# Cached attention with a token mixer: each bulk load split by columns over the SyncE and ScalarE queues

## The chip, the cores and the metric

The kernel runs on one core of a Trainium2 chip. The metric is the device time of one execution in microseconds (us); the time of a kernel is the median of several executions. Beside it stands one profiled execution, from which every duration here is taken. Its span runs from the first to the last recorded instruction.

## What is computed

One decoding step of grouped-query attention over caches of keys and values, plus a token-mixing MLP, plus the input itself. All data is 32-bit float.

```
x: (8, 1, 512)     k_cache, v_cache: (8, 8, 8192, 128)     wq: (512, 4096)     wo: (4096, 512)
xn = layernorm(x)
q  = (xn @ wq) as (8, 32 heads, 1, 128)          # four heads share one key/value head
p  = softmax(q . k * 128**-0.5)
A  = concat(p . v) @ wo
B  = w2 . gelu(layernorm(xn) . w1 + b1) + b2     # S = 1: 1792 hidden units for each of the 512 channels
out = x + A + B
```

The caches hold 64 pairs (batch, key/value head); the kernel works on two of them at a time. A "pair load" of K or V is 128 rows of 64 KB, 8.39 MB; there are 32 of K and 32 of V, and 8.39 MB each of `wq` and `wo`.

## The kernel before

**Buffers.** One tile `raw` holds five slots of 32 KB in each of 128 rows (`RING`). K of step n takes two neighbouring slots: slots 1 and 2 for an even n, 0 and 1 for an odd n (`home`, line 103; steps 0 and 1 differ). V takes slots 3 and 4. In the last step V goes into slots 2 and 1 as two loads, `wo`'s low half into slot 0 and its high half into slot 3.

**A step.** For each of K's two slots, `score_half` (line 420) lets VectorE transpose it in place (`turn`, line 293) and TensorE multiply it with the queries (`scores`, line 302). `softmax_and_values` (line 427) then runs: TensorE multiplies the *previous* step's probabilities with its V (`values`, line 340) around a maximum and an exponential of the current scores (`exps`, ScalarE, line 322), V of the current step is asked for, and `send_on` (line 328) turns the probabilities. `take` (line 347) copies the finished sums from PSUM to `ob` on ScalarE; `place` (line 361) picks the wanted blocks from `ob` on TensorE. In the loop (14 rounds of two steps), each step also runs four Gelus of the mixer on ScalarE (line 394), with their weighting on GpSimd (lines 397 to 400).

**Order.** The schedule is written by hand: each engine runs its instructions in the order in which the Python code issues them. All bulk loads are begun by SyncE (`load`, line 122; `load_wo`, line 143; `wq` at line 97). SyncE has no other work in the program but the store of the result. A load waits, on the engine that begins it, until its slots are free.

**Semaphores of loads.** The framework deals eight semaphores (`DMAHW0` to `DMAHW7`) in turn to the loads of the program, one to each; a load that is dealt a semaphore again waits until the load that had it before has landed, where no earlier wait says so already. A load in the loop has its own, and V of the odd steps counts on a semaphore of the kernel, `landed`, which TensorE waits for (line 430).

**The end.** The code of the last step, whose parts the change touches:

```python
    load(vc, n, 1, 1)
    load_wo(0)
    softmax_and_values(n, lambda: load_wo(1))
    take(n - 1)
    total(HALF)
    place(OT[HALF:, :, final], HALF, 0, 1)
    sums = ps_a.tile([P, D], F32, name="acc")
    values(LAST, 0)
```

`load_wo(1)` begins five loads of 8, 4, 2, 1 and 1 of the 32 chunks of `wo` (a chunk is 128 rows of 2 KB, 0.26 MB). After `values(LAST, 1)`, `take` and `place` of the last step, TensorE multiplies 28 chunks (line 512), ScalarE copies the sums (line 514), TensorE adds the last four chunks (line 520), VectorE copies the result (line 527), and SyncE stores it.

Of the kernel before, what the change touches and what calls it, by code (L numbers as in the profile page):

```python
# [51 lines left out]
def attn_mixer_kernel(ctx: ExitStack, tc: tile.TileContext, x, kc, vc, wq, wo, w1, b1, w2, b2, out):  # L52
    nc = tc.nc
# [10 lines left out]
    def slot(at, n=1):  # L64
        return slots[:, at:at + n, :]
# [12 lines left out]
    def misc():  # L78
        return ps_m.tile([P, 512], F32, name="misc")
# [10 lines left out]
    nc.scalar.dma_start(x_sb, x.rearrange("b s d -> (b s) d"))  # L90
    b2t = const.tile([B, 1], F32, name="b2t")
    nc.scalar.dma_start(b2t, bass.AP(tensor=b2.tensor, offset=b2.offset, ap=[[0, B], [1, 1]]))
    body = slot(2, 2).rearrange("p s m -> p (s m)")
    rows = wq.rearrange("(p e) n -> p (e n)", p=P)
    for a in range(2):
        half = slice(a * QE * QN // 2, (a + 1) * QE * QN // 2)
        nc.sync.dma_start(body[:, half], rows[:, half])
    nil = const.tile([P, 1], F32, name="nil")
    nc.vector.memset(nil, 0.0)

# [10 lines left out]
    landed = tc.alloc_semaphore("landed")  # L111

    def load(c, i, at, part=None, own=False):
        flat = pairs[id(c)]
        if isinstance(i, int):
            rows = flat[i].rearrange("(p m) -> p m", p=P)
        else:
            rows = flat[bass.ds(i, 1)].rearrange("a (p m) -> p (a m)", p=P)
        n = 1 if part is not None else 2
        if part is not None:  # L120
            rows = rows[:, part * SIZE:(part + 1) * SIZE]
        d = nc.sync.dma_start(slot(at, n).rearrange("p s m -> p (s m)"), rows)
        if own:
            d.then_inc(landed, 16)
            tc.no_tile_sem_insts.add(d.ins.name)
            tc.add_to_no_dep_group("landed", d.ins)
        return d

    def tile_at(a):
        return slots[:, a, :].rearrange("p (t d) -> p t d", d=DH)  # L130
# [6 lines left out]
    def load_wo(high):  # L137
        t = slot(3 if high else 0).rearrange("p s (c n) -> p (s c) n", n=D)
        rows = wo.rearrange("(p c) n -> p c n", p=P)
        at = 0  # L140
        for n in WO_HIGH if high else (NWO // 2,):
            o = high * NWO // 2 + at
            nc.sync.dma_start(t[:, at:at + n], rows[:, o:o + n])  # L143
            for c in range(n):
                WO[o + c] = t[:, at + c]
            at += n
# [5 lines left out]
    for k in range(2):  # L152
        load(kc, 0, k, k)
# [22 lines left out]
    m = misc()  # L176
# [16 lines left out]
    rows = tmp[:, :2 * REP]  # L193
# [7 lines left out]
    for k in range(2):  # L201
        for a in range(NB):
            o = a * W + a // 2 * HW
# [3 lines left out]
    for c in range(NCH):  # L207
        for s in range(2):
            o = s * HW + c * REP
# [20 lines left out]
    for k in range(PER):  # L230
        js = slice(k * MJ, (k + 1) * MJ)
        for t, src in ((tabs[:, k::PER, 0], w1t), (tabs[:, k::PER, 1], b1t), (tabw[:, k::PER], w2t)):
            n = len(range(k, ROUNDS, PER))
# [9 lines left out]
    for k in range(2):  # L243
        t = const.tile([P, CH_T * W + W], F32, name=f"pt{k}")
# [12 lines left out]
    def q_project():  # L257
        ms = [misc(), misc()]
        for e in range(QE):
            for h in range(HKV):  # L260
                g = h % NB
                nc.tensor.matmul(ms[h // NB][g * W:(g + 1) * W, :], lx[:, e, :],  # L262
                                 body[:, e * QN + h * REP * DH:e * QN + (h + 1) * REP * DH],
                                 start=(e == 0), stop=(e == QE - 1))
        load(kc, 1, home(1))
        load(vc, 0, 4, 0)
        for a in range(2):
            q = big()
            nc.scalar.copy(q, ms[a])
            mt = misc()  # L270
            for r in range(REP):
                nc.tensor.transpose(mt[:, r * P:(r + 1) * P], q[:, r * DH:(r + 1) * DH], ident)
            nc.vector.tensor_copy(QT[:, a * NB:(a + 1) * NB].rearrange("p g b r -> p r g b"),
                                  mt.rearrange("p (r g x) -> p r g x", r=REP, x=W)[:, :, :, :B])
# [32 lines left out]
    def top(n):  # L307
        mr = work.tile([P, 1], F32, name="mr")
        nc.vector.tensor_reduce(mr, SD[n], AX.X, ALU.max)  # L309
        return mr  # L310

    def exps(n, mr):
        m = misc()
        nc.tensor.transpose(m[:, :P], mr.to_broadcast([P, P]), ident)  # L314
        t = big()[:, :P]
        nc.vector.tensor_tensor(t, m[:, :P], hmask, op=ALU.add)  # L316
        nb = work.tile([P, 1], F32, name="nb")
        nc.vector.tensor_reduce(nb, t, AX.X, ALU.max)
        ns = work.tile([P, 1], F32, name="ns")
        nc.vector.tensor_scalar(ns, nb, -SCALE, None, op0=ALU.mult)  # L320
        p = big()
        nc.scalar.activation(p, SD.pop(n), AF.Exp, bias=ns, scale=SCALE, accum_out=lr[:, n % PER:n % PER + 1])  # L322
        return p

    def send_on(p):
        for k in range(2):
            m = misc()
            nc.tensor.matmul(m, send[:, k, :], p, start=True, stop=True)  # L328
            nc.vector.transpose(PT[k][:, :CH_T * W], m)  # L329

    def apart(d):
        tc.declare_no_dep(d.ins, group="landed", across_iterations=True, reason="waits on landed instead")

    def values(n, k, own=False):
        if not k:
            OD[n] = ps_a.tile([P, 512], F32, name="acc")
        v = tile_at(VAT.get(n, (3, 4))[k]).rearrange("p (c t) d -> p t c d", c=NCH)
        for t in range(CH_T):
            j = t % NB
            d = nc.tensor.matmul(OD[n][j * W:(j + 1) * W, :].rearrange("p (c d) -> p c d", c=NCH),  # L340
                                 PT[k][:, t * W:(t + 1) * W], v[:, t],
                                 start=(not k and t < NB), stop=(k == 1 and t >= CH_T - NB))
            if own:
                apart(d)

    def take(n):
        nc.scalar.copy(OB[:, n % PER, :], OD.pop(n))  # L347
# [79 lines left out]
    def softmax_and_values(n, then, ready=None):  # L427
        mr = top(n)
        if ready is not None:
            nc.tensor.wait_ge(landed, 16)  # L430
            nc.tensor.sem_inc(landed, -16)
        if n:
            values(n - 1, 0, ready is not None)
        p = exps(n, mr)
        if n:
            values(n - 1, 1, ready is not None)
        d = then()
        if ready is not None:
            apart(d)
        send_on(p)  # L440

# [3 lines left out]
    score_half(1, True)  # L445
    load(kc, 2, home(2))
    softmax_and_values(0, lambda: None)
    warm()

    score_half(1, False)  # L450
    softmax_and_values(1, lambda: load(vc, 1, 3))
    nc.tensor.sem_inc(landed, 16)
    take(0)
    total(0)
    q_set(FIRST)
# [5 lines left out]
    with tc.For_i(0, ROUNDS, 1, iteration_sync=SYNC) as r:  # L461
        for k in range(PER):
            n = FIRST + k
            score_half(n, True)
            load(kc, r * PER + (n + 1), home(n + 1))
            score_half(n, False)
            softmax_and_values(n, lambda: load(vc, r * PER + n, 3, own=(k == PER - 1)), k == 0 or None)
            take(n - 1)
            if not k:
                place(RES[:, :, bass.ds(r, 1)], 0)  # L470
                mx_end(r * B)
                mx_begin(r)
                mx_now(r)
            else:
                total(0)
                q_set(r * PER + 2 * FIRST)
            for j in range(k * MIX[0], k * MIX[0] + MIX[k]):
                mx_step(j)
            warm()

    final = slice((B - 1) * BS, (B - 1) * BS + 1)
    n = LAST - 1
# [11 lines left out]
    n = LAST  # L494
    score_half(n, True)
    load(vc, n, 2, 0)
    score_half(n, False)
# [5 lines that stand above are left out]
# [7 lines left out]
    for c in range(FOLD):  # L510
        o = c % NB * W
# [44 lines left out]
```

## Time and profile before

| | us |
|---|---|
| median of 3 executions (lowest, highest) | 1285.84 (1285.82, 1285.96) |
| the profiled execution | 1286.04 |
| its span | 1284.2 |
| TensorE matmuls busy | 767.5 |
| VectorE busy | 696.9 |
| ScalarE busy | 228.8 |
| GpSimd busy | 248.1 |
| bytes moved | 553.86 MB, 431 GB/s over the span |

The profiled execution is 1.84 us longer than its span (work before the first and after the last record), and 0.20 us above the median. Busy times of the engines overlap each other; the transfers run on 16 DMA engines, of which the profile gives the mean busy share.

### The profile page before, as it was taken

To read this page: it belongs to the slowest core of one execution; us is meant where nothing else is said; L and a number is where in the kernel's file an instruction comes from. 1 tells how busy PE (TensorE), PEld (TensorE's weight loads), DVE (VectorE), ACT (ScalarE), POOL (GpSimd) and SP (SyncE) were. 2 spreads that over 40 slices of the span, in tenths; PEclk is the share of its full clock that TensorE was granted. 3 is DMA by queue.
4 is the path that set the end of the run, shared out by engine and by line. 5 is a ranking of instruction groups with operands and counts; after the bars stand their busy time and mean duration, and the time that the engine had idled before them with its cause. 6 is when DMAs were issued, how large, how long until landed. Compare 5 with 4: busy or idle time off the path is not lost. (4 is left out here: it accounts for less than half of the span.)

```text
span 1284.2 us, 13214 instructions
## 1 busy us (share of the span) xinstructions
PE 767.5 (60%) x4830; PEld 170.9 (13%) x4830; DVE 696.9 (54%) x615; ACT 228.8 (18%) x382; POOL 248.1 (19%) x244
## 2 busy tenths in 40 slices
PE   4367556576465665556666475765656665464677
PEld 1111111111011111111111011110111110011112
DVE  3666644466654465644466554565644466543661
ACT  0000221212222121221212222121221211222000
POOL 1000221202222022221212222022221212222000
PEclk8788787887777897788787777877778887778888
DMA  9999999999999999999999999999999999999998
GB/s 409 425 442 425 448 427 433 445 429 433 425 447 429 431 447 427 433 433 439 431 429 447 427 433 445 429 433 427 445 431 429 447 427 433 439 433 431 430 431 354
DMA packets 10975, 553.86 MB, mean 431 GB/s; under 512 B 1324, under 2 KB 1356, under 8 KB 1748
## 3 DMA queue, kind: packets, MB, share of 16 engines
q1 hardware_dynamic: 10836, 553.67, 99.6%
q8 instruction: 8, 0.13, 0.0%
q10 hardware_dynamic: 32, 0.02, 0.0%
q0 software_dynamic: 96, 0.02, 0.0%
q14 instruction: 3, 0.02, 0.0%
HBM read 553.69 MB, written 0.02 MB: 431 GB/s over the span
## 5 line engine op out<-in xcount | busy, mean ns | idle before, releaser
L293 DVE STREAM_TRANSPOSE raw<-raw 128x2048 f32<-128x2048 f32 x256 | 565.4, 2275 | 232.8 <-DMA raw<-in_A_k_cache_dram 218.6
L302 PE MATMUL acc<-raw,z 128*32 128x512 f32 x2048 | 372.8, 815 | 433.9 <-DVE raw L293 385.7
L340 PE MATMUL acc<-raw,pt 128*32 128x512 f32 x2048 | 245.5, 621 | 10.9 <-DMA raw<-in_A_v_cache_dram 5.5
L399 POOL TENSOR_TENSOR g<-g,noww 128x512 f32<-128x512 f32 x98 | 101.8, 1039 | 376.2 <-ACT g L394 376.2
L302 PEld LDWEIGHTS acc<-raw,z 128*32 128x32 f32 x2048 | 47.0, 124 | 737.7 <-DVE raw L293 550.9
L322 ACT ACTIVATE t2k<-acc,ns 128x512 f32<-128x512 f32 x32 | 22.0, 687 | 603.2 <-PE acc L340 525.5
L394 ACT ACTIVATE g<-hb,nows 128x512 f32<-128x512 f32 x112 | 87.5, 782 | 192.8 <-POOL macc L400 175.4
L329 DVE STREAM_TRANSPOSE pt<-misc 128x512 f32<-128x512 f32 x64 | 45.9, 717 | 126.0 <-PE misc L328 121.6
L397 POOL TENSOR_TENSOR macc<-g,noww 128x512 f32<-128x512 f32 x14 | 14.5, 1038 | 515.8 <-ACT g L394 515.8
L400 POOL TENSOR_TENSOR macc<-macc,g 128x512 f32<-128x512 f32 x84 | 106.4, 1267 | 6.6
L340 PEld LDWEIGHTS acc<-raw,pt 128*32 128x32 f32 x2048 | 66.0, 114 | 174.7 <-issue 150.0
L316 DVE TENSOR_TENSOR t2k<-misc,hmask 128x128 f32<-128x128 f32 x32 | 9.3, 292 | 114.8 <-PE misc L314 114.8
L328 PE MATMUL misc<-t2k,send 128*128 128x512 f32 x128 | 65.1, 632 | 3.1 <-ACT t2k L322 3.1
L394 ACT ACT_TABLE_LOAD x28 | 35.9, 1283 | 94.5 <-PE hb L385 94.3
L309 DVE TENSOR_REDUCE mr<-acc 128x1 f32<-128x512 f32 x32 | 22.1, 690 | 52.9 <-PE acc L302 52.9
L409 ACT ACT_TABLE_LOAD x28 | 35.9, 1283 | 0.5
L347 ACT COPY ob<-acc 128x512 f32<-128x512 f32 x32 | 18.7, 585 | 74.3 <-PE acc L340 74.3
L328 PEld LDWEIGHTS misc<-t2k,send 128*128 128x128 f32 x128 | 22.0, 191 | 45.2 <-issue 41.9
L405 PE MATMUL misc<-macc,esel 128*8 128x512 f32 x30 | 15.3, 590 | 19.6 <-DVE esel L403 19.6
L385 PE MATMUL hb<-hn,hsel 8*128 8x512 f32 x28 | 18.9, 761 | 12.9 <-DVE hsel L384 12.9
L406 DVE TENSOR_TENSOR yrow<-misc,yrow 8x512 f32<-8x512 f32 x16 | 10.9, 679 | 19.2 <-PE misc L405 19.2
L262 PE MATMUL misc<-raw,lend 128*32 128x512 f32 x64 | 12.5, 953 | 11.3 <-DMA raw<-in_A_wq_dram 11.3
(99 smaller groups left out, 195.4 us busy)
## 6 DMA issues: line engine op xcount, KB each, us to landing
raw<-in_A_v_cache_dram SPq DMA_DIRECT2D x4, 4096.0 KB, 34.3
raw<-in_A_wq_dram SPq DMA_DIRECT2D x2, 4096.0 KB, 17.0
raw<-in_A_k_cache_dram SPq DMA_DIRECT2D x2, 4096.0 KB, 30.8
raw<-in_A_wo_dram SPq DMA_DIRECT2D x1, 4096.0 KB, 26.4
raw<-in_A_wo_dram SPq DMA_DIRECT2D x1, 2048.0 KB
raw<-in_A_wo_dram SPq DMA_DIRECT2D x1, 1024.0 KB, 29.9
raw<-in_A_wo_dram SPq DMA_DIRECT2D x1, 512.0 KB
raw<-in_A_wo_dram SPq DMA_DIRECT2D x2, 256.0 KB, 30.8
```

The source lines that it names most:

```text
L293: nc.vector.transpose(t, t)
L302: nc.tensor.matmul(SD[n][c * W:(c + 1) * W, :].rearrange("p (t j) -> p t j", j=W), Z[:, n % PER, q, (1 - k) * REP:(1 - k) * REP + W], t[:, ...
L309: nc.vector.tensor_reduce(mr, SD[n], AX.X, ALU.max)
L322: nc.scalar.activation(p, SD.pop(n), AF.Exp, bias=ns, scale=SCALE, accum_out=lr[:, n % PER:n % PER + 1])
L328: nc.tensor.matmul(m, send[:, k, :], p, start=True, stop=True)
L329: nc.vector.transpose(PT[k][:, :CH_T * W], m)
L340: d = nc.tensor.matmul(OD[n][j * W:(j + 1) * W, :].rearrange("p (c d) -> p c d", c=NCH), PT[k][:, t * W:(t + 1) * W], v[:, t], start=(not ...
L385: nc.tensor.matmul(hb, hsel.to_broadcast([B, P]), hn, start=True, stop=True)
L394: nc.scalar.activation(g, hb7 if last else hb, AF.Gelu_apprx_tanh, bias=nows[:, 1, j:j + 1], scale=nows[:, 0, j:j + 1])
L399: nc.gpsimd.tensor_tensor(g, g, w, op=ALU.mult)
L400: nc.gpsimd.tensor_add(acc7 if last else acc, acc7 if last else acc, g)
L409: nc.scalar.activation(small.tile([P, 1], F32, name="warm"), nil, AF.Exp)
```

## The change

Each bulk load becomes two loads of half of its columns, for all 128 rows. The first half is begun by SyncE, the second by ScalarE, by a new helper:

```diff
+    def begin(dst, src):
+        n = dst.shape[1] // 2
+        return [eng.dma_start(dst[:, x], src[:, x]) for eng, x in ((nc.sync, slice(0, n)), (nc.scalar, slice(n, 2 * n)))]
...
-        nc.sync.dma_start(body[:, half], rows[:, half])
+        begin(body[:, half], rows[:, half])
...
-        d = nc.sync.dma_start(slot(at, n).rearrange("p s m -> p (s m)"), rows)
-        if own:
+        ds = begin(slot(at, n).rearrange("p s m -> p (s m)"), rows)
+        for d in ds if own else ():
...
-            nc.sync.dma_start(t[:, at:at + n], rows[:, o:o + n])
+            begin(*(x.rearrange("p c n -> p (c n)") for x in (t[:, at:at + n], rows[:, o:o + n])))
...
-            nc.tensor.wait_ge(landed, 16)
-            nc.tensor.sem_inc(landed, -16)
+            nc.tensor.wait_ge(landed, 32)
+            nc.tensor.sem_inc(landed, -32)
```

For a pair load, half of the columns is one slot: SyncE loads the lower slot, ScalarE the upper one. Lines of the changed kernel below the helper are four higher (`take` is at 351), and the loads all have line 95.

ScalarE at the end of the program, before (the last two steps; `t2k` are probabilities, `ob` what `take` writes):

```order
L322 ACTIVATE t2k,lr<-acc,ns 128x512 [waits DVE_49,PE_49,Activation_49]
L347 COPY ob<-acc 128x512 [waits PE_49]
L409 ACTIVATE warm<-nil 128x1
L322 ACTIVATE t2k,lr<-acc,ns 128x512 [waits DVE_49,PE_49]
L347 COPY ob<-acc 128x512 [waits PE_49,Activation_49] x2
L514 COPY t2k<-acc 128x512 [waits DVE_49,PE_49]
```

The same place in the changed kernel, from the last step's V loads on:

```order
L95 DMA raw<-in_A_v_cache_dram 128x4096 [waits DMAHW1_49]
L95 DMA raw<-in_A_v_cache_dram 128x4096 [waits DMAHW5_49,DVE_49,PE_49]
L95 DMA raw<-in_A_wo_dram 128x4096 [waits DMAHW4_49,DVE_49,PE_49]
L326 ACTIVATE t2k,lr<-acc,ns 128x512 [waits DVE_49]
L95 DMA raw<-in_A_wo_dram 128x2048 [waits DMAHW7_49,DMAHW6_49,PE_49]
L95 DMA raw<-in_A_wo_dram 128x1024 [waits DMAHW1_49]
L95 DMA raw<-in_A_wo_dram 128x512 [waits DMAHW3_49]
L95 DMA raw<-in_A_wo_dram 128x256 [waits DMAHW6_49]
L95 DMA raw<-in_A_wo_dram 128x256 [waits DMAHW7_49]
L351 COPY ob<-acc 128x512 [waits PE_49,Activation_49] x2
L518 COPY t2k<-acc 128x512 [waits DVE_49,PE_49]
```

Eight loads now stand among ScalarE's instructions there. The second halves of `load_wo(1)` stand between the last exponential and the two `take` copies, and four of them wait for a DMA semaphore alone.

TensorE at the end of the kernel before, from the `place` that reads the first of those two copies:

```order
L361 MATMUL misc<-ob,pick 32x128 [waits DVE_49,Activation_49]
L361 MATMUL misc<-ob,pick 32x128 x3
L340 MATMUL acc<-raw,pt_190 32x512 [waits DMAHW5_49]
L340 MATMUL acc<-raw,pt_190 32x512 x15
L506 MATMUL acc<-yrow,spread 32x512
L340 MATMUL acc<-raw,pt_192 32x512 [waits DMAHW6_49,DVE_49]
```

and of the changed kernel:

```order
L365 MATMUL misc<-ob,pick 32x128 [waits DVE_49,Activation_49]
L365 MATMUL misc<-ob,pick 32x128 x3
L344 MATMUL acc<-raw,pt_194 32x512 [waits DMAHW1_49,DMAHW0_49]
L344 MATMUL acc<-raw,pt_194 32x512 x15
L510 MATMUL acc<-yrow,spread 32x512
L344 MATMUL acc<-raw,pt_196 32x512 [waits DMAHW3_49,DMAHW2_49,DVE_49]
L344 MATMUL acc<-raw,pt_196 32x512 x15
L365 MATMUL misc<-ob,pick 32x128 [waits Activation_49]
L365 MATMUL misc<-ob,pick 32x128 x3
L516 MATMUL acc<-raw,ot 32x512 [waits DMAHW4_49,DVE_49]
L516 MATMUL acc<-raw,ot 32x512 x7
L516 MATMUL acc<-raw,ot 32x512 [waits DMAHW5_49]
```

Nothing moved on TensorE; what changed is what its rows wait for. The rows also show how the semaphores were dealt: 0 and 1 to the last V's first part, 2 and 3 to its second part, 4 and 5 to the low half of `wo`. The next rows wait for 6 and 7 (the 8 chunks), 0 and 1 (the 4 chunks), 2 and 3 (the 2 chunks), and 4, 6, 5, 7 (the single ones).

In the loop, ScalarE's round before begins with the even step's exponential, `take` and the mixer's tables (`nows`):

```order
L322 ACTIVATE t2k,lr<-acc,ns 128x512 [waits PE_I-451_own,DVE_I-451_own,Activation_I-451_own,Activation_49]
L347 ISA
L347 COPY ob<-acc 128x512 [waits PE_I-451_own,Activation_I-451_own]
L388 ISA
L388 COPY nows<-tabs 128x16 [waits Activation_I-451_own,Pool_49]
```

and in the changed kernel:

```order
L95 DMA raw<-in_A_k_cache_dram 128x8192 [waits DMAHW1_I-460_own,DVE_I-460_own,DMAHW5_I-460_own,PE_I-460_own,DMAHW0_49]
L326 ISA
L326 ACTIVATE t2k,lr<-acc,ns 128x512 [waits PE_I-460_own,DVE_I-460_own,Activation_I-460_own,Activation_49]
L95 ISA
L95 DMA raw<-in_A_v_cache_dram 128x8192 [waits DMAHW3_I-460_own,PE_I-460_own,DMAHW3_49]
L351 REGISTER_ALU
L351 COPY ob<-acc 128x512 [waits Activation_I-460_own]
```

The upper half of the next K stands ahead of the exponential, the upper half of V between it and `take`; the Gelus and the table loads follow. The odd step has the same order.

More of the change, by code (lines that the diff above doesn't have):

```diff
@@ L126, in load @@
             tc.add_to_no_dep_group("landed", d.ins)
-        return d
+        return ds
     def tile_at(a):
@@ L436, in softmax_and_values @@
             values(n - 1, 1, ready is not None)
-        d = then()
-        if ready is not None:
+        ds = then()
+        for d in ds if ready is not None else ():
             apart(d)
@@ L451, in attn_mixer_kernel @@
     softmax_and_values(1, lambda: load(vc, 1, 3))
-    nc.tensor.sem_inc(landed, 16)
+    nc.tensor.sem_inc(landed, 32)
     take(0)
```

## Prediction

> **What bounds the kernel now.** I read the page's DMA lines first, then busy time by stretches, then the chain of waits' end. The page:
>
> ```profile
> DMA  9999999999999999999999999999999999999998
> ...
> q1 hardware_dynamic: 10836, 553.67, 99.6%
> ...
> L293 DVE STREAM_TRANSPOSE raw<-raw 128x2048 f32<-128x2048 f32 x256 | 565.4, 2275 | 232.8 <-DMA raw<-in_A_k_cache_dram 218.6
> ```
>
> SyncE's queue q1 keeps the 16 DMA engines busy for 99.6% of the span, from the first slice to the last. VectorE, the first to touch a K load, waits 218.6 us for them. So the engines wait for transfers, and the compute is hidden under them. One round of the loop (two steps) as a stretch, the last number being GB/s, and SyncE's issues in one round, then the two places around it:
>
> ```profile
> 1000.00:1077.30 77.30, 46.22 (x298) 9.97 (x290) 42.81 (x36) 15.37 (x25) 17.32 (x16) 0.81 1.00 434
> ```
>
> ```profile
> 575.74 0.33 SPq L122 DMA_DIRECT2D raw<-in_A_k_cache_dram  x1
> 594.27 0.33 SPq L122 DMA_DIRECT2D raw<-in_A_v_cache_dram  x1
> 614.08 0.33 SPq L122 DMA_DIRECT2D raw<-in_A_k_cache_dram  x1
> 653.01 0.33 SPq L122 DMA_DIRECT2D raw<-in_A_k_cache_dram  x1
> ```
>
> A round takes 653.01 - 575.74 = 77.27 us for four pair loads, 19.3 us each at 434 GB/s. How early the queue is filled:
>
> ```profile
> raw<-in_A_k_cache_dram SPq DMA_DIRECT2D x31, 28.2
> ```
>
> A K load lands 28.2 us after its issue; 19.3 us of that is its own transfer, so about 9 us of earlier transfers still stand in the queue at each issue. That is the reserve by which an issue may be late before the DMA engines run dry.
>
> The last part of the chain that ended last, in order of time:
>
> ```profile
> 1249.57 30.87 DMA raw<-in_A_wo_dram
> 1280.44 0.04 issue
> ```
>
> The last piece of `wo` lands at 1280.44, and 3.8 us later the span (1284.2) ends. The transfers bound the kernel up to there, and very little compute is left behind them.
>
> **The change part by part.** *Rate of the loop.* Bytes stay the same; rows halve from 64 to 32 KB. The trace has loads of 32 KB rows: the two loads of K at step 0.
>
> ```profile
> 32.44 8.89 DVE L293 STREAM_TRANSPOSE raw<-raw 128x2048 f32<-128x2048 f32 x4 [17.87 <-DMA raw<-in_A_k_cache_dram]
> 42.09 8.89 DVE L293 STREAM_TRANSPOSE raw<-raw 128x2048 f32<-128x2048 f32 x4 [0.28 <-DMA raw<-in_A_k_cache_dram]
> ```
>
> VectorE was released by the first at 32.44 and by the second at 42.09: 9.65 us for 4.19 MB, 434.6 GB/s, the rate of the 64 KB rows. So the smaller rows and the more frequent completions cost nothing that shows. Two queues busy at once are in no stretch of this trace. A gain is bounded by the 0.4% that q1 leaves, 0.4% of 1284.2 = 5.1 us; I take the same for a loss, and zero as the value, since the row that is nearest shows the same rate. The Trainium skill (DMA: Bandwidth & Descriptors, section Where 436 GB/s comes from) gives a ceiling of 435.2 GB/s for these transfers, which by estimate leaves 1284.2 x (1 - 434/435.2) = 3.5 us to be gained, not 5.1.
>
> *ScalarE as an issuer in the loop.* ScalarE in the round shown above:
>
> ```profile
> 569.08 0.20 ACT L409 ACTIVATE warm<-nil 128x1 f32<-128x1 f32 x1
> 594.25 0.58 ACT L347 COPY ob<-acc 128x512 f32<-128x512 f32 x1 [1.90 <-PE acc L340]
> 613.34 0.20 ACT L409 ACTIVATE warm<-nil 128x1 f32<-128x1 f32 x1
> ```
>
> ScalarE's last work of a step ends at 569.28, 6.5 us before K's slots were free (575.74), and at 613.54, 0.5 us before 614.08. Its K halves can thus be begun no later than SyncE began the whole load. V's half stands behind the exponential, which waits for scores anyway, and ahead of `take`, which waits for the same `values` as the load. SyncE's halves come earlier than before: the lower K slot of an odd step is free since the step before, and the lower V slot after the first half of `values`. With equal turns both queues stay filled; no gap arises, and none was there to close. The cost is 0.33 us of issue ahead of each `take`; what waits for `take` in an even step is `place`, then VectorE's turn of the next K:
>
> ```profile
> 603.93 17.66 DVE L293 STREAM_TRANSPOSE raw<-raw 128x2048 f32<-128x2048 f32 x8 [3.87 <-DMA raw<-in_A_k_cache_dram]
> ```
>
> VectorE stood 3.87 us idle for K there, which hides 0.33. Uncovered it would be 28 x 0.33 = 9 us. Loop: 0.
>
> *The start.* The first loads on ScalarE stand ahead of the square root of the layer norm, and one of them (K of step 0, upper slot, second half) is dealt the semaphore of the first piece of `wq`, so it waits until that has landed.
>
> ```profile
> 3.61 0.29 ACT L167 ACTIVATE sd<-mv,epst 8x1 f32<-8x1 f32 x1 [0.65 <-DVE mv L165]
> 13.40 6.06 PE L262 MATMUL misc<-raw,lend 128*32 128x512 f32 x32 [7.98 <-DMA raw<-in_A_wq_dram]
> 22.80 6.47 PE L262 MATMUL misc<-raw,lend 128*32 128x512 f32 x32 [3.34 <-DMA raw<-in_A_wq_dram]
> ```
>
> Half of `wq` had landed by 13.40, and a quarter no later. The root then starts at about 15 instead of 3.61, and the query projection about 2 us behind it, at 17, not 13.40; it ends its first half at about 23.2, and the second, held by `wq` until 22.80 anyway, 0.4 us later than before. K's next load is queued until 42 at least, so 0.4 us is hidden. Start: 0.
>
> *The end.* Here a wait is added whose cover I can't find. SyncE's queue shows how a waiting load treats what is behind it:
>
> ```profile
> 1.66 28.01 SPq L122 DMA_DIRECT2D raw<-in_A_k_cache_dram  x3
> 29.71 21.53 SPq L122 DMA_DIRECT2D raw<-in_A_v_cache_dram  x2
> ```
>
> The third K load waits for the projection, and the V load behind it, whose slot 4 nothing had used, begins only at 29.71. A load that waits holds its engine's later instructions. The Trainium skill (Perfetto Trace Analysis, section DMA Instruction — HWDGE) puts a load's wait on the issuing sequencer ahead of its next decode, and the row agrees.
>
> By ScalarE's order at the end, the two single-chunk halves wait for semaphores 6 and 7. The holders of these before them are the halves of the 8 chunks. Behind them stand both `take` copies. The first `take` releases TensorE's `place`, and behind that on TensorE stands all the rest: both parts of the last `values`, the projection with `wo`, the sum. When do the 8 chunks land? Rows of the end:
>
> ```profile
> 1251.58 0.58 ACT L347 COPY ob<-acc 128x512 f32<-128x512 f32 x1 [1.91 <-PE acc L340]
> 1254.28 3.60 PE L340 MATMUL acc<-raw,pt 128*32 128x512 f32 x29
> 1257.81 1.04 PE L506 MATMUL acc<-yrow,spread 8*32 8x512 f32 x2
> 1261.14 5.12 PE L340 MATMUL acc<-raw,pt 128*32 128x512 f32 x32 [2.29 <-DMA raw<-in_A_v_cache_dram]
> 1266.38 0.58 ACT L347 COPY ob<-acc 128x512 f32<-128x512 f32 x1 [14.22 <-PE acc L340]
> 1267.02 1.06 PE L361 MATMUL misc<-ob,pick 128*32 128x128 f32 x8 [0.76 <-ACT ob L347]
> 1268.92 0.21 DVE L367 TENSOR_TENSOR ot<-s,rl 32x32 f32<-32x32 f32 x1
> 1270.80 8.24 PE L512 MATMUL acc<-raw,ot 128*32 128x512 f32 x56 [2.72 <-DMA raw<-in_A_wo_dram]
> ```
>
> ```profile
> L143 SPq DMA_DIRECT2D raw<-in_A_wo_dram x6: 327/440/458, 1244.3 to 1249.6; - x6
> ```
>
> The low half of `wo` landed at 1270.80, the last of the 16 high chunks at 1280.44, so 8 of them take 4.82 us: 1275.62. However the queues share, both halves of these 8 land no earlier than 4.82 us before all transfers end, since only 8 chunks follow them. Two issues of 0.44 us follow: the first `take` begins at 1276.6 instead of 1251.58. From there, with no transfer left to wait for:
>
> `take` to the end of `place` takes 1.70 (1266.38 to 1268.08). The first part of `values`, on a TensorE that idled for over 20 us, takes 5.33 by the first row below; the row above has 3.60 for 29 when it had been working. Line 506 takes 1.0, the second part of `values` 3.64, also below. `take`, `place` and VectorE's steps of the last V take 2.87 (1266.26 to 1269.13). Line 512 has 56 at the pace of 29 in 3.60, 6.95. From its end to the span's end it is 5.16 as before (1279.04 to 1284.2).
>
> ```profile
> 584.89 5.33 PE L340 MATMUL acc<-raw,pt 128*32 128x512 f32 x32 [0.76 <-PEq L431]
> 1247.82 3.64 PE L340 MATMUL acc<-raw,pt 128*32 128x512 f32 x32
> ```
>
> Sum: 1276.6 + 1.70 + 5.33 + 1.0 + 3.64 + 2.87 + 6.95 + 5.16 = 1303.3 us of span, 19.1 above before. What was spread over 1251 to 1270 beside the transfers now comes behind them. With 1.84 us around the span and 0.20 down from the profiled execution to the median, the time is 1304.9.
>
> Ends of these terms: both parts at 3.64, line 506 at 0.6, line 512 at 56 x 3.64/32 = 6.4 and 4.9 behind it give 1300.3; 5.33, 5.12, 8.24 and 5.16 give 1306.1. As times 1301.9 and 1307.7.
>
> **The rivals.** *Only transfers count, and the wait holds nothing* (no change). ScalarE would have to pass `take` ahead of waiting loads. For it: the bytes and the rate stay, as in all rows above. Against it: the V load held until 29.71. Time: 1285.84, give or take the 5.1 of the rate. The Trainium skill (DMA: Bandwidth & Descriptors, section Rules for kernel authors) says that spreading loads over issuers doesn't help bandwidth, as all share 16 engines; by that rule alone the time stays, and the 434.6 beside 434 agrees. It decides if `take` begins before 1257.5: from there the 26.7 us of the chain above end at 1284.2.
>
> *Finer release pays* (faster). SyncE's halves are begun earlier and fill q1's missing 0.4%, and the end isn't held: 1285.84 - 5.1 = 1280.7. Against it: both conditions, the second as above; a gain of 5.1 alone leaves 1299.8.
>
> *Two busy queues cost rate* (slower still). The one stretch in which ScalarE's and GpSimd's small loads ran beside SyncE's:
>
> ```profile
> 2.00:12.00 10.00, 0.61 (x4) 0.55 (x4) 7.76 (x39) 1.26 (x2) 2.22 (x6) 1.00 0.96 402
> ```
>
> 402 against 434 GB/s, though the first loads' latency is in it. If that held throughout, transfers would take 8% or 102 us more: 1407. Against it: 0.04 MB of small loads can hardly slow 4 MB by themselves.
>
> **How the numbers follow.** The held `take`: 0.88; no change: 0.03; faster: 0.02; a lost rate beyond 0.4%: 0.07. Forecast 1304.9. Range: 1301.9 and 1307.7, widened by 5.1 either way: 1297 to 1313. Changes within 0.2% (2.6 us) can't be told from none here. Slower 0.95, same 0.03, faster 0.02.
>
> **What would show it.** Right: the round still takes 77.3 us; the first `take` of the end (line 351) starts near 1276 with the single-chunk halves on ScalarE just before it; TensorE has a gap of over 20 us from about 1254 on; DMA share falls to nothing in the last 23 us of the span; the chain that ended last runs through ScalarE's queue into lines 365, 344 and 516. Wrong: `take` still near 1252; rounds off 77.3 by over 0.3 us; or waits of VectorE for K that grow while the DMA share falls.

## The result and the profile after

The changed kernel takes 1307.32 us (median of four executions, 1305.95 to 1308.32), the kernel before beside it 1285.83 (1285.70 to 1285.96): a ratio of 1.0166, with a 95% interval of 1.0149 to 1.0184. That is 21.5 us more. The profiled execution took 1307.2 us, its span 1305.4.

The page of the changed kernel, its DMA lines and two groups (busy time and mean on the left of the last bar, idle time before them and its cause on the right):

```profile
DMA  9999999999999999999999999999999999999992
GB/s 401 431 437 434 433 433 434 434 432 433 434 432 433 434 432 434 433 433 434 434 433 432 433 433 434 434 434 434 434 434 434 434 434 434 434 433 433 431 424 119
...
q1 hardware_dynamic: 10836, 276.85, 49.2%
q10 hardware_dynamic: 10832, 276.85, 49.2%
...
L297 DVE STREAM_TRANSPOSE raw<-raw 128x2048 f32<-128x2048 f32 x256 | 565.4, 2275 | 191.2 <-DMA raw<-in_A_k_cache_dram 176.6
...
L365 PE MATMUL misc<-ob,pick 128*32 128x128 f32 x256 | 19.0, 280 | 22.1 <-ACT ob L351 22.1
```

The bytes are split evenly over SyncE's queue (q1) and ScalarE's (q10), and together they need twice as many packets, 21668 for the same 553.7 MB. The DMA engines stay busy until the last slice, which was 8 before and is 2 now, so most of that slice (32.6 us wide) has no transfers. VectorE's idle time for K is less than before (176.6 us, it was 218.6), although the kernel is longer: it isn't where the time went. The idle time of `place` (line 365), 22.1 us behind ScalarE's copy, is where an engine shows the loss.

The bulk of the program as one stretch, before and then after (the last number is GB/s):

```profile
121.00:1180.00 1059.00, 637.09 (x3996) 137.59 (x3995) 580.70 (x482) 212.14 (x346) 236.62 (x219) 0.80 1.00 434
```

```profile
121.00:1180.00 1059.00, 645.77 (x3972) 139.07 (x3964) 580.55 (x481) 210.47 (x344) 233.57 (x215) 0.80 1.00 433
```

One GB/s is the last digit shown, so I went to SyncE's issues of even-step K loads twelve rounds apart, before and then after:

```profile
227.74 0.33 SPq L122 DMA_DIRECT2D raw<-in_A_k_cache_dram  x1
...
1155.02 0.33 SPq L122 DMA_DIRECT2D raw<-in_A_k_cache_dram  x1
```

```profile
227.64 0.33 SPq L95 DMA_DIRECT2D raw<-in_A_k_cache_dram  x1
...
631.25 0.33 SPq L95 DMA_DIRECT2D raw<-in_A_v_cache_dram  x1
632.38 0.33 SPq L95 DMA_DIRECT2D raw<-in_A_k_cache_dram  x1
...
1157.05 0.33 SPq L95 DMA_DIRECT2D raw<-in_A_k_cache_dram  x1
```

Twelve rounds took 927.28 us before and 929.41 after: 77.27 and 77.45 us a round, 0.23% more. By these loads a single round before takes anything from 76.39 to 78.16 us, but three together take 231.79 to 231.84, and 232.35 or 232.36 after, so the difference is clear of this spread. The two rows in the middle show that SyncE begins the lower K slot of an odd step 1.13 us behind a V load, early, as the code says; the rounds are no shorter for it.

The end of the changed kernel as a timeline (start, duration, engine, line; in brackets the idle time before and what ended it):

```profile
1253.83 0.33 ACTq L95 DMA_DIRECT2D raw<-in_A_wo_dram  x1
...
1255.76 23.32 ACTq L95 DMA_DIRECT2D raw<-in_A_wo_dram  x4
...
1258.22 0.23 PE L357 MATMUL misc<-lr,ohg 128*32 128x1 f32 x4
...
1279.17 0.59 ACT L351 COPY ob<-acc 128x512 f32<-128x512 f32 x1 [24.65 <-DMA raw<-in_A_wo_dram]
...
1279.81 1.27 PE L365 MATMUL misc<-ob,pick 128*32 128x128 f32 x5 [21.37 <-ACT ob L351]
...
1281.52 5.18 PE L344 MATMUL acc<-raw,pt 128*32 128x512 f32 x29
...
1287.59 3.64 PE L344 MATMUL acc<-raw,pt 128*32 128x512 f32 x32
...
1291.36 0.59 ACT L351 COPY ob<-acc 128x512 f32<-128x512 f32 x1 [11.60 <-PE acc L344]
...
1294.16 6.21 PE L516 MATMUL acc<-raw,ot 128*32 128x512 f32 x56 [1.10 <-DVE ot L371]
```

ScalarE begins the half of the 8 chunks at 1253.83 and needs from 1255.76 to 1279.08 to begin the four loads behind it. Only then does `take` start, at 1279.17; before, it started at 1251.58. TensorE stands from 1258.45 to 1279.81. The chain that ended last, at that place:

```profile
1253.83 24.89 DMA raw<-in_A_wo_dram
1278.74 0.33 ACTq L95
1279.17 0.60 ACT ob L351
```

It names the wait: the half of the 8 chunks lands at 1278.74, the last single-chunk load, which was dealt the same semaphore, is begun then, and `take` follows 0.43 us later. Nobody reads those 8 chunks before 1294.16. Two stretches of the end (busy time of TensorE, its weight loads, VectorE, ScalarE and GpSimd; then the clock granted to TensorE, with 1.00 for full speed, DMA share, GB/s):

```profile
1260.00:1279.00 19.00, 0.00 (x0) 0.00 (x0) 0.00 (x0) 0.00 (x0) 0.00 (x0) 0.52 1.00 423
1284.00:1305.40 21.40, 15.81 (x159) 5.59 (x151) 1.16 (x4) 1.17 (x2) 0.00 (x0) 0.98 0.01 2
```

For 19 us no engine computes while transfers run; then for 21.4 us the engines compute while no transfers run. The two used to lie over each other.

### The profile page after: what moved, and what is told of

The parts are those of the page before. It is cut to its first block, busy times and chain, and to the rows that moved or that the text cites. A ratio compares the mean times of both kernels' runs of the same rounds, so it can differ in the third digit from the quotient of the medians.

```text
span 1305.4 us, 13503 instructions
## 1 busy us (share of the span) xinstructions
PE 778.9 (60%) x4830; PEld 173.4 (13%) x4830; DVE 696.9 (53%) x615; ACT 228.8 (18%) x382; POOL 248.3 (19%) x244
## 2 busy tenths in 40 slices
DMA packets 21776, 553.88 MB, mean 424 GB/s; under 512 B 2524, under 2 KB 3068, under 8 KB 3588
## 3 DMA queue, kind: packets, MB, share of 16 engines
q1 hardware_dynamic: 10836, 276.85, 49.2%
## 5 line engine op out<-in xcount | busy, mean ns | idle before, releaser
L297 DVE STREAM_TRANSPOSE raw<-raw 128x2048 f32<-128x2048 f32 x256 | 565.4, 2275 | 191.2 <-DMA raw<-in_A_k_cache_dram 176.6
L344 PE MATMUL acc<-raw,pt 128*32 128x512 f32 x2048 | 260.2, 652 | 33.8 <-DMA raw<-in_A_v_cache_dram 28.5
L313 DVE TENSOR_REDUCE mr<-acc 128x1 f32<-128x512 f32 x32 | 22.1, 690 | 51.6 <-PE acc L306 51.6
L365 PE MATMUL misc<-ob,pick 128*32 128x128 f32 x256 | 19.0, 280 | 22.1 <-ACT ob L351 22.1
L368 DVE TENSOR_TENSOR t2k<-misc,keep 64x128 f32<-64x128 f32 (+1 forms) x17 | 4.8, 284 | 36.7 <-PE misc L365 36.7
```

Source lines behind the costliest of these rows:

```text
L297: nc.vector.transpose(t, t)
L365: nc.tensor.matmul(m[at + k * W:at + (k + 1) * W, :DH], pick[:, c, :], OB[:, k, c * DH:(c + 1) * DH], start=(c == 0), stop=(c == NCH - 1))
```

## The experiments

**The theory:** some 18 us are the held `take`, and what is left over, about 3 us, is lost in the transfers. **The rivals:** the loss comes from two queues that disturb each other; or it comes from the finer release of slots or from ScalarE's issues in the loop. For the 3 us there were further candidates: shorter rows (more packets), or more loads. Every kernel below ran beside the kernel before, which took 1286.08 beside the first three and the kernel with one queue, 1286.39 beside the three with fewer pieces and the one with the 64-byte gap, and 1285.95 beside the 1 KB gap and the last two.

### Both halves kept, but nothing of the end waits on ScalarE

Here only `load_wo(1)` changes against the changed kernel; all other loads stay halved over both engines.

```diff
-            begin(*(x.rearrange("p c n -> p (c n)") for x in (t[:, at:at + n], rows[:, o:o + n])))
+            if high:
+                nc.sync.dma_start(t[:, at:at + n], rows[:, o:o + n])
+            else:
+                begin(*(x.rearrange("p c n -> p (c n)") for x in (t[:, at:at + n], rows[:, o:o + n])))
```

> The change, but the high half of wo is again five whole loads begun by SyncE, so no load stands among ScalarE's instructions between the last exponential and the two take copies. Theory A (the held take costs about 19 us, the two queues themselves 0.2% of rate): take starts near 1256, a median of about 1288.5. Theory B (two queues, smaller rows or more loads cost 1.6% of the rate throughout): about 1306, with take near 1279 or the loop's rounds over 78 us. Theory C (the held take is all): 1286.

Measured: 1288.93, ratio 1.0022 (1.0013 to 1.0031). The first `take` in the timeline, and the end of the chain:

```profile
1258.60 0.59 ACT L354 COPY ob<-acc 128x512 f32<-128x512 f32 x1 [1.97 <-PE acc L347]
```

```profile
1262.88 20.49 DMA raw<-in_A_wo_dram
1283.37 0.04 issue
```

`take` waits for TensorE again, and the kernel ends with its transfers, at 1283.37 where they ended at 1280.44 before. Of the 21.5 us, 18.6 are gone (21.49 less 2.85).

### All loads and waits kept, but `take` moved off ScalarE

The edit above also removes loads. This one leaves each load where it is and moves the two last copies to VectorE.

```diff
-    def take(n):
-        nc.scalar.copy(OB[:, n % PER, :], OD.pop(n))
+    def take(n, vector=False):
+        (nc.vector.tensor_copy if vector else nc.scalar.copy)(OB[:, n % PER, :], OD.pop(n))
...
-    take(n - 1)
+    take(n - 1, True)
...
-    take(LAST)
+    take(LAST, True)
```

> The change with all its loads and waits, but the two take copies of the end run on VectorE, which has no loads in its queue. Theory A: the waits of the single-chunk halves stay, but nothing stands behind them that TensorE needs before 1283; the first copy starts near 1256, a median of about 1289 (0.2% of rate, and the last single-chunk halves land about 3 us late as they are begun late). Theory B: about 1307, the chain's end is moved only by the rate.

Measured: 1289.28, ratio 1.0025 (1.0015 to 1.0035). From its timeline:

```profile
1255.54 23.42 ACTq L95 DMA_DIRECT2D raw<-in_A_wo_dram  x4
...
1259.91 0.65 DVE L351 COPY ob<-acc 128x512 f32<-128x512 f32 x1
...
1261.52 3.60 PE L344 MATMUL acc<-raw,pt 128*32 128x512 f32 x29
```

ScalarE's queue stands as long as in the changed kernel, 23.42 us, and it costs nothing, since nothing needed stands behind it until the sums are copied at 1282.15. So neither the wait nor the second queue is the price: what stood behind the wait was.

### The kernel before, with only that wait added

```diff
+    nc.scalar.copy(small.tile([P, 1], F32, name="hold"), WO[NWO // 2][:, :1])
     take(n - 1)
```

One small copy on ScalarE reads the first of the 8 chunks, and so can't start before they have landed. No load is touched.

> The kernel before, all loads whole and on SyncE, plus one ScalarE copy of one column (0.2 us) out of the 8 chunks of wo, put ahead of the first take of the end, so that take waits for those 8 chunks. Theory A: they land at 1275.6 as worked out from the trace of before; take starts at 1275.9, and with the 26.2 us from take to the end that the changed kernel showed the span is 1302.1, the median 1303.7. Theory B (the loss is in the two queues): 1286, as the chain would be hidden again.

Measured: 1304.18, ratio 1.0137 (1.0122 to 1.0153).

```profile
1276.41 0.19 ACT L501 COPY hold<-raw 128x1 f32<-128x1 f32 x1 [25.23 <-DMA raw<-in_A_wo_dram]
1276.51 0.58 ACT L347 COPY ob<-acc 128x512 f32<-128x512 f32 x1
```

The wait alone costs 18.1 us. With the 3.2 us that the kernel with `take` on VectorE keeps, that makes 21.3 of the 21.5.

### Fewer pieces, so that the last load waits for something earlier

If the dealt semaphore is the cause, the number of pieces sets what the last one waits for. With pieces of 8 and 8 the last half has the semaphore of the last V's first part; with 8, 4, 4 that of V's second part; with 8, 4, 2, 2 that of the low half of `wo`; with the changed kernel's five that of the 8 chunks.

```diff
-WO_HIGH = (8, 4, 2, 1, 1)
+WO_HIGH = (8, 8)
```

> The change with the high half of wo in two pieces of 8 chunks instead of five (8, 4, 2, 1, 1). ScalarE's last half then waits for the semaphore of the last V's first part, which by the changed kernel's trace lands about three times 8 chunks and two parts ahead of 1278.7, near 1254.6. Theory A: take is not held (about 1258.6, as with the high half whole), and the end pays only for a last piece of 8 chunks: the transfers end at 1283.5, then 4 chunks of line 516 (1.2 us) and 5.2 us: span 1289.9, median about 1291.5. If the number of loads or the queue's order were the cost instead of the held take: 1305 to 1307.

> The change with the high half of wo in pieces of 8, 4 and 4 chunks. ScalarE's last half waits for the last V's second part, which lands near 1264.3. Theory A: take at 1264.8, and 26.2 us from there to the end: span 1291.0, median about 1292.6. A theory in which the hold is hidden up to some point would put it at 1289.

> The change with the high half of wo in pieces of 8, 4, 2 and 2 chunks. ScalarE's last half waits for the low half of wo, which lands near 1274.0. Theory A: take at 1274.5, span 1300.7, median about 1302.3. Any theory without the held take: as with 8, 4, 4 or lower.

Measured, in this order: 1291.64, ratio 1.0039 (1.0024 to 1.0055); 1293.78, ratio 1.0057 (1.0041 to 1.0072); 1302.79, ratio 1.0131 (1.0115 to 1.0146). The first `take` with 8 and 8:

```profile
1257.71 0.59 ACT L351 COPY ob<-acc 128x512 f32<-128x512 f32 x1 [1.97 <-PE acc L344]
```

with 8, 4, 4 (the last load just before it):

```profile
1264.95 0.33 ACTq L95 DMA_DIRECT2D raw<-in_A_wo_dram  x1
1265.38 0.58 ACT L351 COPY ob<-acc 128x512 f32<-128x512 f32 x1 [9.60 <-DMA raw<-in_A_v_cache_dram]
```

and with 8, 4, 2, 2:

```profile
1255.64 18.83 ACTq L95 DMA_DIRECT2D raw<-in_A_wo_dram  x3
...
1274.57 0.58 ACT L351 COPY ob<-acc 128x512 f32<-128x512 f32 x1 [20.38 <-DMA raw<-in_A_wo_dram]
```

The releaser in the brackets changes from TensorE to V to `wo`, as the deal has it. From the start of `take` to the end of the span it is 25.9 us with 8, 4, 4 (span 1291.3), 26.4 with 8, 4, 2, 2 (1301.0), 26.2 in the changed kernel and 26.5 with the wait alone (1303.0). Where `take` starts late, the end follows it at nearly the same distance. With 8 and 8 it isn't held, and the chain of that kernel goes through its last load:

```profile
1254.19 28.41 DMA raw<-in_A_wo_dram
1282.61 0.04 issue
```

7.4 us of its span (1290.0) come after that landing, where 3.8 did before: the last piece is 8 chunks, with more work behind it. That its time met the 1291.5 expected is in part luck: the landing came 0.9 us earlier than the 1283.5 expected, and the work behind it took 1.0 more than 6.4. The size for 8, 4, 4 was 1.2 us off, within the spread of its executions (1291.47 to 1295.02).

### Where the other 3 us come from: one queue

```diff
-        return [eng.dma_start(dst[:, x], src[:, x]) for eng, x in ((nc.sync, slice(0, n)), (nc.scalar, slice(n, 2 * n)))]
+        return [eng.dma_start(dst[:, x], src[:, x]) for eng, x in ((nc.sync, slice(0, n)), (nc.sync, slice(n, 2 * n)))]
```

> The change, but SyncE begins both halves of every load: as many loads and rows as the change, one queue, ScalarE without loads. Theory A: no held take, so 1286 to 1289: near 1288.5 if the lost 0.2% of rate comes with the number of loads or the 32 KB rows, near 1286 if it comes with two queues that take turns. Theory B: 1306 if it is the rows or the number of loads, 1286 if it is the two queues; B and A are then told apart by the run with the held take alone.

Measured: 1289.20, ratio 1.0024 (1.0014 to 1.0033), the same as with two queues.

```profile
q1 hardware_dynamic: 21636, 553.67, 99.7%
```

The second queue is not the cause of the 3 us, nor does it gain anything; and as ScalarE begins none of the bulk loads here, its issues in the loop are not the cause either. The Trainium skill (DMA: Bandwidth & Descriptors, section Issuing engines are not separate DMA queues) says that loads from any engine share the same 16 DMA engines and that spreading them saves only issue time. For the rate the runs agree: 1289.20 on one queue, 1288.93 and 1289.28 on two. The time of the kernel did change with the issuer: the wait that came with ScalarE as the second one cost 18 us.

### Short rows without more loads

The kernel before with a gap between neighbouring slots, so that each pair load is still one load by SyncE but moves two rows of 32 KB in each of the 128 rows of `raw`. The gap is 64 bytes in the first kernel and 1 KB in the second (`+ 256`). Not shown: `wq`, which lies across two slots, is addressed slot by slot.

```diff
-    slots = ring.tile([P, RING, NT * DH], F32, name="raw")
+    slots = ring.tile([P, RING, NT * DH + 16], F32, name="raw")[:, :, :NT * DH]
...
-        d = nc.sync.dma_start(slot(at, n).rearrange("p s m -> p (s m)"), rows)
+        d = nc.sync.dma_start(slot(at, n), rows.rearrange("p (s m) -> p s m", s=n))
```

> The kernel before with 64 bytes of unused columns between the slots, so that each pair load is one load of rows of twice 32 KB instead of 64 KB, begun by SyncE; as many loads as before. It asks where the 3 us of rate go that stayed when the take was not held. If the smaller rows cost them: about 1289, and 433 GB/s in the loop. If the number of loads (and of their completions) does: 1286 and 434.

> As the kernel before with a gap between the slots (rows of twice 32 KB, one load each), but with a gap of 1024 bytes instead of 64. With 64 bytes it took 4.7 us more for 7808 packets more, where the two column halves on SyncE took 3.1 for 10800. If the odd offset of 64 bytes took part in it: below 1289, with 2.2 us or less for the packets; if not: 1291 again.

Measured: 1291.04, ratio 1.0039 (1.0025 to 1.0053), with 64 bytes; 1288.19, ratio 1.0017 (1.0008 to 1.0026), with 1 KB. The queue reads the same in both:

```profile
q1 hardware_dynamic: 18644, 553.67, 99.7%
```

The page counts 18644 - 10836 = 7808 packets more, 488 on each of 16 DMA engines. With as many loads as before, the same waits and no finer release of slots, the kernel with the 1 KB gap takes 2.24 us more, 4.6 ns for each of the 488. The kernel with all halves on SyncE has 10800 more, 675 on each engine, and 3.12 us: 4.6 ns too. So the price of shorter rows is enough to account for the 3 us of the change, and more loads need not be blamed. This is agreement within wide limits, and no proof: the intervals of the two ratios allow 2.1 to 6.9 ns and 2.7 to 6.3 ns, and of the 10800 packets 1200 are under 512 bytes (the pages count 2524 such packets, and 1324 before), of which the kernels with a gap have no more than the kernel before. Nor is the price the same everywhere: the 64-byte gap costs 4.65 us, 9.5 ns a packet, with the same packets, where about 3 us were expected. Of the two programs only the places of the buffers differ; why that costs so much is open.

### Four quarters, and halves by rows

Four quarter-column loads, all by SyncE, the high half of `wo` whole:

```diff
-        n = dst.shape[1] // 2
-        return [eng.dma_start(dst[:, x], src[:, x]) for eng, x in ((nc.sync, slice(0, n)), (nc.scalar, slice(n, 2 * n)))]
+        n = dst.shape[1] // 4
+        return [nc.sync.dma_start(dst[:, x * n:(x + 1) * n], src[:, x * n:(x + 1) * n]) for x in range(4)]
```

> Every load but the high half of wo as four loads of a quarter of the columns, all begun by SyncE (rows of 16 KB, four times the loads). With both halves on SyncE the loss was 3.1 us for about 10800 packets and 64 loads more. If the loss grows with packets or loads: three times as many more, 9.3 us, 1295.4. If it was a fixed loss of splitting at all: 1289.

Measured: 1295.19, ratio 1.0070 (1.0057 to 1.0082). The queue, and the same stretch as above:

```profile
q1 hardware_dynamic: 41076, 553.68, 100.1%
```

```profile
121.00:1180.00 1059.00, 653.07 (x3955) 146.38 (x3955) 579.54 (x475) 207.46 (x336) 233.97 (x215) 0.80 1.01 431
```

That is 30240 packets more, 1890 on each engine, for 9.24 us: 4.9 ns each (3.9 to 5.6 by the interval). The cost grows with the packets, or with the loads, of which there are four times as many; a fixed price of splitting, which would have given 1289, is out. The Trainium skill (DMA: Bandwidth & Descriptors, section Why small descriptors are slow) gives about 3 cycles of overhead for each packet, with an example of 256 bytes. It doesn't say of which clock; at the 850 MHz that the Trainium skill (the same page, section Where 436 GB/s comes from) states for the fabric, that is by estimate 3.5 ns. The runs show 4.6 to 4.9, at rows of 32 and 16 KB, and their intervals don't rule out 3.5 at 32 KB.

Two loads of 64 rows with all columns, both by SyncE, against the kernel before, were to give twice the loads at the old row length:

```diff
+    def begin(dst, src):
+        return [nc.sync.dma_start(dst[x], src[x]) for x in (slice(0, HALF), slice(HALF, P))]
```

> Every load as two loads of 64 rows each and all columns, both begun by SyncE: as many loads as the change, rows as long as before. If the lost 3 us of rate come with the number of loads (their completions): about 1289, as with both column halves on SyncE. If they come with the 32 KB rows alone: 1286. If a load of only 64 rows can't use all of the 16 DMA engines' paths, the time is far above both, and the run tells nothing on this question.

Measured: 2674.35, ratio 2.0787 (2.0757 to 2.0818). The queue, and a stretch in the middle:

```profile
q1 hardware_dynamic: 12036, 553.67, 99.9%
```

```profile
1000.00:1100.00 100.00, 27.79 (x157) 6.24 (x161) 24.97 (x22) 8.01 (x13) 9.62 (x10) 0.62 1.00 206
```

Half the rate, with the DMA engines shown as busy throughout. So it can't say what more loads cost, and that question rests on the gap of 1 KB alone.

None of these kernels beats the kernel before, and none points to one that would: it ends 3.8 us behind its transfers, and every kernel with more packets made those longer.

## Why the prediction was right, point by point

*What bounds the kernel.* Held. With the end freed (first two experiments) the time follows the transfers again.

*Rate of the loop: zero.* This term was mis-sized, inside its bounds of 5.1 us: a round takes 77.45 us, not 77.27, and the transfers end about 3 us later (12 GB/s from 1283.0 to 1283.5 and none in the half microsecond behind it, where the last piece landed at 1280.44 before). The row that I took for it, 9.65 us for one 4.19 MB load, could not show this: 0.23% of it is 0.02 us, one or two units of the last digit, in a single sample. Twelve rounds can.

*ScalarE as an issuer in the loop: nothing.* Held: with ScalarE as an issuer and the end freed the time is 1288.93 or 1289.28, and 1289.20 without ScalarE's loads. One detail was otherwise. ScalarE in the changed kernel:

```profile
611.88 0.78 ACT L398 ACTIVATE g<-hb,nows 128x512 f32<-128x512 f32 x1 [2.50 <-POOL macc L404]
612.11 0.34 ACTq L95 DMA_DIRECT2D raw<-in_A_k_cache_dram  x1
612.68 1.28 ACT L413 ACT_TABLE_LOAD   x1
```

The K load is begun while a Gelu runs, and ahead of the table load that stands before it in the code. A load goes out when ScalarE's sequencer reaches it, and the sequencer runs ahead of the engine; the page of the profile writes the two as ACTq and ACT.

*The start: nothing.* Held. ScalarE and then VectorE in the changed kernel:

```profile
2.67 8.32 ACTq L95 DMA_DIRECT2D raw<-in_A_k_cache_dram  x2
11.02 1.28 ACT L171 ACT_TABLE_LOAD   x1 [11.02 <-DMA raw<-in_A_wq_dram]
12.31 0.29 ACT L171 ACTIVATE sd<-mv,epst 8x1 f32<-8x1 f32 x1
```

```profile
36.21 8.89 DVE L297 STREAM_TRANSPOSE raw<-raw 128x2048 f32<-128x2048 f32 x4 [12.92 <-DMA raw<-in_A_k_cache_dram]
```

The root is held by `wq`, as the deal of semaphores had it, and starts at 12.31; I had said about 15. The first half of K comes 3.8 us later (32.44 before). The kernel with all halves on SyncE has no such hold:

```profile
32.82 8.89 DVE L297 STREAM_TRANSPOSE raw<-raw 128x2048 f32<-128x2048 f32 x4 [17.51 <-DMA raw<-in_A_k_cache_dram]
```

It is no faster (1289.20) than the first experiment (1288.93), where this row starts at 36.17. So the late start is hidden.

*The end: `take` held until the 8 chunks have landed.* Held, mechanism and size. The 8 chunks landed at 1278.74, not 1275.62: 3.1 us, the transfers' delay. Of the two issues of 0.44 us only one was left behind the wait, so `take` followed after 0.43, not 0.98. From `take` to the span's end it took 26.2 us (1279.17 to 1305.4), not 26.65: up to the second part of `values` 8.4 (8.0 forecast), that part 3.64, the way to line 516 2.9, line 516 6.21 (6.95 forecast, at the pace of 29 in 3.60), and 5.0 behind it. Together 3.1 - 0.55 - 0.4 = 2.1, which is the span's 1305.4 against 1303.3. The rest of the 2.4 us between 1304.9 and 1307.32 is the median, which now lies 0.12 above the profiled execution.

One reading in this sum fitted only in its size. The 5.33 for the first part of `values` was to be that of a TensorE that had stood for over 20 us, but the row it came from had been idle for 0.76 us. What the row shares with the end is the clock: 0.68 while it ran (584.89 to 590.20). The first part of `values` in the changed kernel, and in the kernel with `take` on VectorE:

```profile
1279.80:1286.70 6.90, 6.89 (x41) 3.55 (x42) 0.85 (x3) 0.00 (x0) 0.00 (x0) 0.65 0.37 135
```

```profile
1261.00:1265.10 4.10, 4.10 (x40) 2.18 (x38) 0.86 (x3) 0.00 (x0) 0.00 (x0) 1.00 1.01 432
```

After the gap of 21.4 us the clock was 0.65, and 29 matmuls took 5.18 us; without the gap it was 1.00, and they took 3.60. So about 1.6 us of the 18 go with this clock (2.0 in the kernel before with the wait added, where they took 5.59).

*The rivals.* No change would have asked ScalarE to pass `take` ahead of the waiting loads; it didn't (1279.17, and the limit was 1257.5). Finer release starts loads earlier, and the time without the hold is still 3 us worse. A rate lost to two queues is out by the kernel with one queue. What is lost, 0.2%, goes with the packets by the runs above, and was not among the rivals. The 434.6 beside 434, which I took as agreeing with the rule on issuers, compares two row lengths on SyncE's queue alone and says nothing of issuers; the kernels on one and two queues do.

*What would show it.* The round was to be 77.3 (77.45); `take` near 1276 (1279.17); TensorE's gap over 20 us, from about 1254 (21.4, from 1258.45); transfers gone in the last 23 us (22 by the rate above); the chain through ScalarE's queue into lines 365, 344 and 516: all as said, the times 3 to 4.5 us later. VectorE's waits for K, which would have grown had the forecast been wrong, fell.

## What to carry to other kernels

A load put on an engine that also computes is a wait put ahead of that engine's next instructions, and where semaphores are dealt in turn the wait may be for a load that has nothing to do with it: count which load had the semaphore before, and see what stands behind it in the queue. In this kernel such waits cost nothing at the start and in the loop, and 18 us at the end, where the work that used to lie under the last transfers had nothing left to lie under; moving the held instruction to another engine gave that time back without touching a load. And a price of 0.2% can't be read from one transfer of 9.65 us: take it over many rounds.

## What the runs showed of the hardware that was not expected

- Shorter rows cost time even at 32 and 16 KB: 4.6 to 4.9 ns for each further packet on a DMA engine (but for the 64-byte gap), 0.2% from 64 to 32 KB rows and 0.7% at 16 KB. At 16 KB the loads were four times as many as well.
- A gap of 64 bytes between 32 KB destinations costs twice as much as a gap of 1 KB (4.65 against 2.24 us), with the same packets. Open.
- Two loads of 64 rows in place of one of 128 halve the rate, 206 against 434 GB/s, with the 16 DMA engines 99.9% busy. The Trainium skill (DMA: Bandwidth & Descriptors, section Rules for kernel authors) says that transfers to two halves of the partitions are not worth it because they share the same engines; the runs agree with the advice, and show a loss by a factor of 2.08 that it doesn't mention. What sets it no run here shows.
